# Gated linear attention with an ELU feed-forward: two windows in one visit, four-quadrant products from window 6, loads without the zero rows, and a new issue order of the start

## The chip, the cores and the metric

The kernel runs on one core of a Trainium2 chip. The time is that of the device in microseconds (us) for one execution; a kernel's time is the median of its runs. The core has five engines with queues of their own: TensorE (PE), VectorE (DVE), ScalarE (ACT), GpSimd (POOL) and SyncE (SP), which only issues transfers (DMA) here. Each engine works its instructions in the order in which they were issued, and waits on semaphores for the others.

## The reference

There are 4 batches with 8 heads, 768 steps and a head size of 48. For each head a 48 x 48 state is decayed by a gate per row, gets the outer product of k and v, and is read with q. The outputs of the 8 heads stand side by side as 384 numbers for each of the 3072 tokens, and go through a feed-forward layer with 2048 hidden units.

```python
for t in range(S):
    state = alpha[:, :, t, :, None] * state + np.einsum('bhd,bhe->bhde', k[:, :, t], v[:, :, t])
    y[:, :, t] = np.einsum('bhd,bhde->bhe', q[:, :, t], state)
...
h = x @ w_in
g = np.where(h > 0.0, h, alpha * (np.exp(np.minimum(h, 0.0)) - 1.0))
return (g @ w_out).astype(np.float32)
```

In the second part alpha is 1, so g is the ELU of h.

## The kernel before

**Attention in windows.** The 768 steps of a batch are cut into 6 windows of 128 steps, 24 windows in all. Two heads share the 128 partitions (rows 0 to 47 and 64 to 111; the rows between are zeros), and four such pairs stand side by side, so a window's q, k and gate are one tile of 128 partitions (`qka`), one load (token L; the first two windows in two pieces, LA and LB). A scan on DVE (SC) multiplies the gates up, ACT takes the logarithm and the exponent of it (LN, EX), k and q are scaled (KA, KB, KC, SQ on DVE or POOL). Keys are transposed (TP on PE and KN on ACT in the first windows, T, TA, TB on DVE later). Inside a window there are two chunks of 64 steps. PE computes the scores of each chunk (S), DVE masks them (MK); PE computes the products of keys and values (U), DVE subtracts them from the state (UA, UB) and decays it for the next window (UC); PE computes the outputs y (Y, in the first four windows with YL and Y3), which take both the scores and the state.

**Quarters.** S and U exist in two forms. In the old one a matmul contracts over 128 partitions against operands that hold zeros for the other head (ZS writes such zeros, V0 loads them). In the form with quarters (`S4`, `U4`) four small matmuls work on four 64 x 64 quadrants; each window then has two PSUM banks (`q4`) with U in the first part and S behind it. `QU` and `QS` say from which window the form is used.

**Feed-forward.** Two windows make a block of 256 tokens; there are 12 blocks. y is written to `xt` as a high and a low part in a reduced fp32 form (XH on ACT, XL on DVE; XD is a small transfer that moves the fourth pair's rows). The 2048 hidden units are cut in 8 pieces j. For each block b and piece j, A(b, j) is 18 matmuls of 128x256 into a PSUM bank `h`, ACT and DVE make the ELU (RA, RB, RC) and its high and low part (GH on ACT, GL on DVE), and O(b, j) is 12 matmuls of 128x384 into two banks that are kept over all j; Z copies them out and stores them.

**Weights.** They come as 64-bit words in 16 pieces (F). DVE decodes them (DA, DB, DC, one each for a pair of pieces), ACT writes the high part (WH), DVE or POOL the low part (WL; the list `WLV` says which pieces are DVE's; two pieces go over PE, WP). CA and CB read them again for a check (LC loads). This goes on during the first 70 to 80 us, between the first windows and blocks.

**Order.** Every operation is a token, and the tokens are issued one after the other. `START` is a list, written out by hand, for windows 0 to 9 and for the first three blocks; `steady()` makes the rest from a table of offsets, in which each operation of window i stands at a fixed step n = 4i + offset of the sequence of A's. An engine's queue holds its instructions in that order. All PSUM tiles (eight banks) come from one pool in turn, so a new `h` or a new pair of banks waits until the last reader of the bank's former tile is done. `X.n` are n matmuls on constants whose result is not used; 12 stand ahead of everything.

## Time and profile before

| | |
|---|---|
| median of 3 runs | 513.34 us (511.15 to 514.16) |
| the profiled execution | 510.82 us, span 509.1 us, mean granted clock 0.997 |
| PE busy | 499.0 us, 98% |
| DVE busy | 394.3 us, 77% |
| ACT busy | 301.5 us, 59% |
| POOL busy | 123.2 us, 24% |
| DMA | 61.53 MB in 22724 packets |

The span is the time from the first to the last instruction; the profiled execution's own time is longer by what lies around it. A line in the profile such as `L643 DVE SCALAR_TENSOR_TENSOR h<-r,h ... x96 | 66.1, 693 | 51.1 <-ACT r L638 50.5` is a group: line of the kernel, engine, operation, output and inputs with their shapes, how often; then busy us, mean ns of one; then idle us of the engine just ahead of them and what ended most of it. The chain of waits is the work that ended last, followed back from the end. In the timeline each row has its start, its length and how many equal instructions are in it. The lines on which the prediction rests stand there.

### The profile page before, as it was taken

The numbers are of one execution on the slowest core, as the hardware profiler recorded it, in microseconds if no ns is written. First come the engines' busy times: TensorE is split into PE (matmuls) and PEld (weight loads), VectorE is DVE, ScalarE is ACT, GpSimd is POOL, SyncE is SP. The second block draws the span as 40 slices with busy tenths as digits, with TensorE's granted clock in tenths as the row PEclk, the third lists the DMA queues.
The fourth block names the chain that finished last, engine by engine and source line by source line (L and its number), as shares of the span: only waits on it lengthen the run. The fifth ranks groups of instructions, "written<-read, shape, count | busy, mean of one in ns | idle before, by whom it ended". The sixth has DMA issues, their size and how long they took to land.

```text
span 509.1 us, 13170 instructions
## 1 busy us (share of the span) xinstructions
PE 499.0 (98%) x5404; PEld 482.5 (95%) x5404; DVE 394.3 (77%) x801; ACT 301.5 (59%) x689; POOL 123.2 (24%) x115
## 2 busy tenths in 40 slices
...
GB/s 311 403 410 382 188 1 215 13 120 76 119 102 1 133 148 54 158 121 77 164 102 94 165 79 117 164 72 124 160 74 127 71 66 37 72 40 1 31 4 36
DMA packets 22724, 61.53 MB, mean 121 GB/s; under 512 B 2944, under 2 KB 10112, under 8 KB 22656
## 3 DMA queue, kind: packets, MB, share of 16 engines
...
q8 instruction: 44, 0.72, 0.6%
...
q14 instruction: 24, 0.20, 0.1%
HBM read 53.92 MB, written 4.72 MB: 115 GB/s over the span
## 4 chain that ended last, share of the span: by engine, by line
PE 95%; DMA 3%; SPq 1%; issue 1%; DVE 0%; ACT 0%
PE h L625 41%; PE o L676 40%; PE y L428 4%; DMA vs<-in_vv_dram 3%; PE sc L318 2%; PE q L346 2%; PE u L362 1%; PE y L423 1%; PE q L303 1%; PE wp L112 1%; PE tp L259 0%; SPq L535 0%; PE y L467 0%; PE yl L423 0%; SPq L174 0%
## 5 line engine op out<-in xcount | busy, mean ns | idle before, releaser
L625 PE MATMUL h<-xt,w 128*128 128x256 f32 x1728 | 221.4, 282 | 0.0
L625 PEld LDWEIGHTS h<-xt,w 128*128 128x128 f32 x1728 | 214.0, 188 | 1.5
L676 PE MATMUL o<-w,gh 128*128 128x384 f32 x768 | 198.4, 339 | 0.0
L676 PEld LDWEIGHTS o<-w,gh 128*128 128x128 f32 x768 | 135.6, 188 | 0.2
L676 PE MATMUL o<-w,gl 128*128 128x384 f32 x384 | 129.9, 338 | 0.0
L649 ACT CAST gh<-h 128x512 fp32r<-128x512 f32 x96 | 56.3, 587 | 88.3 <-DVE h L643 71.7
L643 DVE SCALAR_TENSOR_TENSOR h<-r,h 128x512 f32<-128x512 f32 x96 | 66.1, 693 | 51.1 <-ACT r L638 50.5
L633 ACT ACTIVATE r<-h 128x512 f32<-128x512 f32 x96 | 56.7, 594 | 75.1 <-PE h L625 73.5
L238 POOL TENSOR_TENSOR st<-qka,P 64x512 f32<-64x512 f32 x36 | 42.9, 1190 | 212.0 <-issue 166.5
L662 DVE TENSOR_TENSOR gl<-h,gh 128x512 fp32r<-128x512 f32 x96 | 66.1, 690 | 34.2 <-ACT gh L649 33.0
L269 DVE STREAM_TRANSPOSE kn<-qka 32x128 f32<-32x128 f32 x288 | 87.1, 302 | 4.1
L676 PEld LDWEIGHTS o<-w,gl 128*128 128x128 f32 x384 | 72.1, 188 | 0.0
L638 ACT ACTIVATE r<-r 128x512 f32<-128x512 f32 x96 | 60.5, 633 | 2.5
L192 DVE TENSOR_TENSOR_SCAN P<-qka,first 128x516 f32<-128x516 f32 x24 | 29.6, 1237 | 2.3 <-DMA qka<-in_qka_dram 1.5
L214 POOL TENSOR_TENSOR qka<-qka,R 128x512 f32<-128x512 f32 x18 | 23.9, 1330 | 12.5 <-ACT R L206 12.4
L219 POOL TENSOR_TENSOR R<-P,R 128x512 f32<-128x512 f32 x19 | 24.7, 1300 | 5.0 <-DVE qka L214 3.9
L330 DVE TENSOR_TENSOR st<-q,mask 64x256 f32<-64x256 f32 x52 | 22.0, 422 | 1.0
L428 PEld LDWEIGHTS y<-st,vs 128*64 128x64 f32 x576 | 18.3, 138 | 4.2 <-issue 4.0
L581 ACT ACTIVATE ck<-ck,lim 128x384 f32<-128x384 f32 x32 | 20.9, 653 | 1.0
L428 PE MATMUL y<-st,vs 128*64 128x64 f32 x576 | 20.7, 225 | 0.0
L201 ACT ACTIVATE R<-P 128x512 f32<-128x512 f32 x24 | 15.1, 633 | 8.4 <-DVE P L192 8.4
L576 ACT ACTIVATE ck<-ck 128x384 f32<-128x384 f32 x32 | 18.2, 568 | 0.1
(105 smaller groups left out, 418.5 us busy)
## 6 DMA issues: line engine op xcount, KB each, us to landing
...
```

What stands on the lines that cost most here:

```text
L192: nc.vector.tensor_tensor_scan(out=P.rearrange("p n w -> p (n w)"), data0=t[:, 2 * NP * W:], data1=first.rearrange("p n w -> p (n w)"), in ...
L219: eng(KBV, i).tensor_tensor(out=d["R"], in0=pw(i), in1=d["R"], op=ALU.mult)
L238: eng(SQV, i).tensor_tensor(out=st[r, a], in0=d["q"][r], in1=pw(i)[r], op=ALU.mult)
L269: nc.vector.transpose(out=kn[32 * t:32 * t + 32, :, 32 * g:32 * g + 32], in_=d["kt"][32 * g:32 * g + 32, :, 32 * t:32 * t + 32])
L428: nc.tensor.matmul(out[64 * a:64 * a + m], lhsT=lhs(i, c, a)[:, n * D:n * D + m], rhs=d["st"][:, a, n, c * C:(c + 1) * C], start=start, st ...
L625: nc.tensor.matmul(h[:, f, :], lhsT=t[:, wi, ws], rhs=x[:, c, xi, :], start=(f == 0 and k == 0), stop=(k == 8), skip_group_check=True)
L633: nc.scalar.activation(out=r, in_=d["h"], func=AF.Relu, scale=-1.0)
L638: nc.scalar.activation(out=d["r"], in_=d["r"], func=AF.Exp, scale=-1.0)
L643: nc.vector.scalar_tensor_tensor(out=d["h"], in0=d["r"], scalar=-1.0, in1=d["h"], op0=ALU.add, op1=ALU.max)
L649: nc.scalar.copy(out=gh, in_=d["h"])
L662: nc.vector.tensor_tensor(out=gl, in0=d["h"], in1=d["gh"].bitcast(F32), op=ALU.subtract)
L676: nc.tensor.matmul(o[:, 0:DM], lhsT=gt[:, f, ms], rhs=t[:, wi, f * DM:f * DM + DM], start=(j == 0 and f == 0 and k == 0), stop=(j == NJ - ...
```

## The change

Five things are changed together.

- The steady order is a list for one block (`STEADY`) instead of a table of offsets for one window: numbers in it are relative to the block's first A (A.0 of block g) and its first window. Per block there is one visit with y of both windows, and one with U, S, U, S of the next two windows, instead of y, U, S once for each window.
- Quarters start with window 6 instead of 10 for U and 11 for S. S then lies beside its own window's U in one pair of banks from window 10 on (`PAIRS`, `shared`), where before it lay behind U of the window ahead of it.
- From window 3 on a load moves rows 0 to 47 and 64 to 111 only, as two transfers; the three tiles are fixed, and the other rows keep the zeros of windows 0 to 2.
- From window 10 on, every fourth window's masked scores lie in the buffer in which the weights were decoded.
- `START` has a new order for windows 0 to 9, and it reaches further, to O.3.2 instead of O.2.6. Two of WL's pieces, one KA, one KB and one SQ go from DVE to POOL. Both `X.2` are gone.

```diff
--- before.py
+++ after.py
@@ -32,9 +32,11 @@
 WARM = 12
 
 
-QU, QS, SHARE = 10, 11, 11
-
-WLV, KAV, KBV, SQV = (1, 3, 9, 10, 12), (0, 1, 3, 6, 7, 10), (0, 1, 2, 3, 8), (1, 3, 4, 5)
+QU, QS = 6, 6
+
+PAIRS = 10
+
+WLV, KAV, KBV, SQV = (6, 11, 14), (0, 1, 2, 3, 4), (0, 1, 2, 3), (0, 1, 3)
 
 
 WPE, XPE, GPE, UPE = (0, 2), (0, 1), (), (1,)
@@ -43,32 +45,44 @@
 
 
 START = """
-LA.0 SC.0 X.2 LB.0 LN.0 EX.0 LA.1 SQ.0 LB.1 KA.0 KB.0 SC.1 SQ.1 F.0 F.2 KC.0 LN.1 EX.1 LV.1 KA.1 LV.0 S.0 KB.1
-TP.0 KC.1 L.2 PC.0 TP.1 KN.1 KN.0 L.3 PC.1 DA.0 DB.0 S.1 DC.0 U.0 WH.0 U.1 UC.0 X.2 UA.0 UP.1 SC.2 WP.0 F.6
-WH.2 LN.2 SQ.2 MK.1 F.4 LV.3 F.1 UC.1 SC.3 UA.1 EX.2 MK.0 WP.2 DA.2 F.3 YL.1 KA.2 L.5 YL.0 LV.2 KB.2 KC.2 F.9
-LN.3 Y3.1 Y.1 EX.3 DB.2 Y3.0 KA.3 PC.2 KB.3 Y.0 WL.0 XH.1 LC.0 S.2 F.11 TP.2 XP.1 XH.0 KN.2 XP.0 SQ.3 KC.3
-DC.2 TP.3 DA.1 U.2 XL.1 KN.3 U.3 DB.1 WL.2 DC.1 WH.4 UB.2 XL.0 F.5 S.3 L.4 PC.3 A.0.0 UA.2 WH.6 WH.1 UC.2 F.10
-A.0.1 CA.0 WL.6 A.0.3 MK.2 UB.3 UA.3 WH.3 MK.3 UC.3 WL.4 RA.0.0 YL.2 F.7 LV.5 RB.0.0 YL.3 RA.0.1 Y3.2 SC.4
-WL.1 Y3.3 F.12 SC.5 SQ.4 DA.3 WL.3 LN.5 Y.2 LN.4 RB.0.1 SQ.5 F.8 Y.3 RC.0.0 EX.4 EX.5 F.14 A.0.2 RC.0.1 XH.3
-XH.2 L.7 XL.3 XL.2 GH.0.0 GH.0.1 KA.4 GL.0.0 DA.5 DB.3 KA.5 KB.5 DC.3 CB.0 LV.7 V0.7 LV.6 V0.6 RA.0.2 RA.0.3
...
+LA.0 SC.0 LN.0 EX.0 LA.1 SC.1 LB.0 LB.1 KA.0 LN.1 EX.1 SQ.0 KB.0 KC.0 KA.1 KB.1 TP.0 F.0 F.2 KC.1 LV.0 SQ.1
+DA.0 S.0 PC.1 LV.1 LV.2 TP.1 DB.0 S.1 KN.1 L.2 PC.0 KN.0 L.3 U.0 DC.0 UC.0 SC.2 F.4 UA.0 WH.0 MK.0 F.6 U.1
+LV.3 UP.1 WP.0 YL.0 MK.1 UC.1 UA.1 LN.2 SC.3 EX.2 Y3.0 YL.1 F.12 KA.2 KB.2 KC.2 Y3.1 Y.0 LN.3 F.3 SQ.2 WH.2
+Y.1 F.1 SQ.3 EX.3 XH.0 KA.3 XP.0 TP.2 PC.2 F.7 XH.1 WP.2 L.4 KN.2 KB.3 KC.3 XL.0 DA.2 XP.1 LV.5 DB.2 F.5 DC.2
+U.2 DA.1 XL.1 WL.0 S.2 L.5 WH.6 A.0.0 F.11 DB.1 UA.2 UB.2 TP.3 MK.2 UC.2 WH.4 SC.4 WL.2 S.3 KN.3 A.0.1 U.3
+DA.3 WL.4 F.10 RA.0.0 F.9 LN.4 RB.0.0 MK.3 UA.3 DC.1 YL.2 Y3.2 A.0.2 YL.3 DB.3 EX.4 DC.3 RA.0.2 KA.4 Y3.3 WL.6
+PC.3 UB.3 WH.1 Y.2 SQ.4 XH.2 RB.0.2 WH.7 KB.4 F.14 Y.3 XH.3 UC.3 A.0.3 KC.4 ZV.6 TP.4 LV.4 SC.5 SQ.5 XL.3 S.4
+KN.4 WH.3 XL.2 DA.5 RC.0.2 F.8 RC.0.0 DB.5 GH.0.2 LN.5 U.4 EX.5 UB.1 L.7 L.6 RA.0.3 WH.5 GL.0.2 WL.1 RA.0.1
...
+"""
+
+
+STEADY = """
+A.-3 Y.1 XH.1 Y.0 XH.0 A.-2 XL.1 RA.-3 O.-5 RA.-2 XL.0 LV.4 U.2 CA.-12 V.0 RB.-3 S.2 UA.2 MK.2.0 U.3 UB.2 S.3
+MK.2.1 UC.2 XD.1 ZV.4 O.-4 XD.0 RC.-3 CB.-12 SC.4 RB.-2 A.-1 PC.3 GH.-3 RC.-2 A.0 LN.4 GL.-3 UA.3 EX.4 RA.-1
+GH.-2 LC.-11 MK.3.0 L.6 MK.3.1 UB.3 CA.-11 A.1 RA.0 KA.4 L.5 RB.-1 GL.-2 RC.-1 A.2 RB.0 UC.3 CB.-11 RA.1 GH.-1
+RC.0 O.-3 KB.4 RB.1 SC.5 KC.4 LC.-10 GL.-1 LN.5 GH.0 EX.5 RC.1 T.4.1 O.-2 A.3 VP.0 CA.-10 T.4.2 GL.0 GH.1 A.4
+T.4.3 KA.5 O.0 RA.2 GL.1 RB.2 RA.3 CB.-10 LV.5 RC.2 PC.4 GH.2 KB.5 RB.3 GL.2 LC.-9 O.1 O.-1 KC.5 RA.4 O.2 SQ.4
+T.5.2 CA.-9 RB.4 RC.3 CB.-9 RC.4 GH.3 T.5.1 GH.4 T.5.0 GL.3 T.4.0 T.5.3 LC.-8 SQ.5 Z.-1 GL.4
 """
 
 @with_exitstack
@@ -149,13 +163,19 @@
         return win[i]["P"][:, :, 1:]
 
 
+    NQ = 3
+    qka_t = [work.tile([128, QW], F32, name=f"qka{i}", tag=f"qka{i}", bufs=1) for i in range(NQ)]
+
     def qtile(i):
-        t = win[i]["t"] = work.tile([128, QW], F32, name="qka", tag="qka", bufs=3)
+        t = win[i]["t"] = qka_t[i % NQ]
         return t
 
+
     @tok
     def L(i):
-        nc.sync.dma_start(out=qtile(i), in_=qka[i, :, 0:QW])
+        t = qtile(i)
+        for r in [slice(0, 128)] if i < NQ else [slice(0, D), slice(64, 64 + D)]:
+            nc.sync.dma_start(out=t[r], in_=qka[i, r, 0:QW])
 
     @tok
     def LA(i):
@@ -230,7 +250,13 @@
     @tok
     def SQ(i):
         d = win[i]
-        st = d["st"] = work.tile([128, 2, NP, W], F32, name="st", tag="st", bufs=3)
+        if i >= PAIRS and i % 4 == 3:
+
+            st = work.tile([128, 2, WCH], F32, name="st", tag="wm", bufs=1)
+            st = st.rearrange("p a x -> p (a x)")[:, 0:2 * NP * W].rearrange("p (a n w) -> p a n w", a=2, n=NP)
+        else:
+            st = work.tile([128, 2, NP, W], F32, name="st", tag="st", bufs=3)
+        d["st"] = st
         if i < EARLY:
             eng(SQV, i).tensor_tensor(out=st[:, 0], in0=d["q"], in1=pw(i), op=ALU.mult)
         for a in range(2 if i >= EARLY else 0):
@@ -288,20 +314,25 @@
         nc.scalar.copy(out=kn, in_=d["tp"].rearrange("p n (a x) -> p n a x", a=2))
 
 
-    def banks(i):
-        return [psa.tile([128, 512], F32, name="q", tag="pa") for _ in range(2)]
+
+    def shared(i):
+        d = win[i]
+        if i < PAIRS or "q4" not in d:
+            d["q4"] = [psa.tile([128, 512], F32, name="q", tag="pa") for _ in range(2)], set()
+        return d["q4"]
 
     QUADS = ((0, 0), (1, 1), (0, 1), (1, 0))
 
     def S4(i):
         d = win[i]
-        q4 = win[i - 1]["q4"] if i >= SHARE else banks(i)
+        q4, begun = shared(i)
         d["s4"] = [t[:, NP * D:NP * (D + C)].rearrange("p (n t) -> p n t", n=NP) for t in q4]
         for n in range(NP):
             for a, c in QUADS:
                 r, cs = slice(64 * a, 64 * a + D), slice(c * C, (c + 1) * C)
                 nc.tensor.matmul(d["s4"][a][64 * c:64 * c + 64, n, :], lhsT=d["kt"][r, n, cs], rhs=d["st"][r, a, n, cs],
-                                 start=(n == 0 and (i < SHARE or a == 1 and i % NW == 0)), stop=True, skip_group_check=True)
+                                 start=(n == 0 and a not in begun), stop=True, skip_group_check=True)
+        begun.update((0, 1))
 
     @tok
     def S(i):
@@ -338,13 +369,15 @@
 
     def U4(i):
         d = win[i]
-        d["q4"] = banks(i)
-        d["u"] = [t[:, 0:NP * D].rearrange("p (n e) -> p n e", n=NP) for t in d["q4"]]
+        q4, begun = shared(i)
+        d["u"] = [t[:, 0:NP * D].rearrange("p (n e) -> p n e", n=NP) for t in q4]
         for n in range(NP):
             for x, a in QUADS if i % NW < NW - 1 else QUADS[::2]:
                 r = slice(64 * x, 64 * x + 64)
                 nc.tensor.matmul(d["u"][x][64 * a:64 * a + 64, n, :], lhsT=d["kn"][r, n, a, :],
-                                 rhs=d["vn"][r, 2 * n + a, :], start=(n == 0), stop=True, skip_group_check=True)
+                                 rhs=d["vn"][r, 2 * n + a, :], start=(n == 0 and x not in begun), stop=True,
+                                 skip_group_check=True)
+        begun.update((0, 1) if i % NW < NW - 1 else (0,))
 
     @tok
     def U(i):
@@ -730,60 +763,29 @@
     general(ctx, tc, ident, [t[:, 0] for t in wgts], [t[:, 1] for t in wgts], flag[0], qka, vn, wgt, out)
 
 
-def steady(n0=25):
-
-
-    LEFT = dict(T=11)
-    p, late = [], [divmod(n, NJ) for n in range(n0 - 2, n0)]
-
-    def at(n, start, *names):
...
-    p, late = [], [divmod(n, NJ) for n in range(n0 - 2, n0)]
-    for n in range(n0, NBLK * NJ):
-        b, j = divmod(n, NJ)
-        at(n, -22, "L", "LV")
-        at(n, -7, "Y")
-        at(n, -11, "U")
-        at(n, -15, "S")
-        p.append(("A", b, j))
...
-        second(*late.pop(0))
...
+def steady(g0=4):
+
+
+    p, steps, last = [], dict(A=29, RA=29, RB=29, RC=29, GH=29, GL=29, O=27), NBLK * NJ
+    for g in range(g0, g0 + 10):
+        for x in STEADY.split():
+            x, k, *y = x.split(".")
+            if x in steps:
+                k = NJ * g + int(k)
+                if steps[x] <= k < last:
+                    p.append((x, *divmod(k, NJ)))
+            elif x in ("CA", "CB", "LC"):
+                k = 4 * g + int(k)
+                if 4 + (x == "LC") <= k < 4 * NJ:
+                    p.append((x, k))
+            elif x == "Z":
+                if g0 - 1 <= g + int(k) < NBLK:
+                    p.append((x, g + int(k)))
+            elif x in ("V", "VP"):
+                if g == NBLK - 1:
+                    p.append((x,))
+            elif 2 * g + int(k) < NWIN:
+                p.append((x, 2 * g + int(k), *map(int, y)))
     return p
 
 
```

`X.2` no longer appears: before it stood twice in `START`, behind SC.0 and behind UC.0.

**The start on PE.** Names: `wd` are the two rounds of a weight's low part (WP.0 and WP.2), `yl` and `y` the outputs of windows 0 and 1, `tp` transposed keys, `sc` scores, `u` state products, `h` the first A. Before, from the end of the second weight round on:

```order
L598 MATMUL wd<-wm,ident 128x384
L486 MATMUL wd<-w_233,minus 128x384
L423 MATMUL yl<-st,vs_106 64x64 x8
L423 MATMUL yl<-st,vs_105 64x64 x6
L467 MATMUL y<-y_319,sel 64x128 x6
L423 MATMUL y<-st,vs_106 48x64 x24
L467 MATMUL y<-y_354,sel 64x128 x6
L423 MATMUL y<-st,vs_105 48x64 x18
L318 MATMUL sc<-st,qka 64x64 x16
L259 MATMUL tp<-ident,qka 128x128 x4
L486 MATMUL y<-xt,minus 128x384 x2
L259 MATMUL tp<-ident,qka 128x128 x4
```

and now, from the end of those y to the first A and behind it:

```order
L456 MATMUL y<-st,vs_106 48x64 x24
L519 MATMUL y<-xt,minus 128x384
L285 MATMUL tp<-ident,qka_125 128x128 x4
L631 MATMUL wd<-wm,ident 128x384
L519 MATMUL wd<-w_238,minus 128x384
L631 MATMUL wd<-wm,ident 128x384
L519 MATMUL wd<-w_238,minus 128x384
L519 MATMUL y<-xt,minus 128x384
L395 MATMUL u<-vs_107,kn 64x48 x16
L349 MATMUL sc<-st,qka_125 64x64 x16
L658 MATMUL h<-xt,w_238 128x256 x18
L285 MATMUL tp<-ident,qka_123 128x128 x4
```

The second weight round moved behind the y groups, and the transposes, scores and products of window 3 moved behind the first A. Before, U and S of windows 2 and 3 and both `tp` stood ahead of it.

**The loads on SP.** `vs_107` is the v of window 2, `raw` are weight pieces, `qka` the windows. Before:

```order
L535 DMA raw_146<-in_wgt_dram 128x1536 x2
L174 DMA vs_106<-in_vv_dram 128x768
L174 DMA vs_105<-in_vv_dram 128x768
L158 DMA qka<-in_qka_dram 128x1540 x2
L535 DMA raw_266<-in_wgt_dram 128x1536 x2
L174 DMA vs_108<-in_vv_dram 128x768
L535 DMA raw_276<-in_wgt_dram 128x1536 x2
L158 DMA qka<-in_qka_dram 128x1540
L174 DMA vs_107<-in_vv_dram 128x768
```

and now:

```order
L568 DMA raw_154<-in_wgt_dram 128x1536 x2
L194 DMA vs_105<-in_vv_dram 128x768
L194 DMA vs_106<-in_vv_dram 128x768
L194 DMA vs_107<-in_vv_dram 128x768
L178 DMA qka_125<-in_qka_dram 128x1540
L178 DMA qka_123<-in_qka_dram 48x1540 x2
```

The v of window 2 now stands right behind those of windows 0 and 1, and window 3's load is two transfers of 48 rows.

**The steady order on PE.** `q` are the banks of U and S with quarters, `y` outputs, `h` an A, `o` an O (twelve matmuls, in the rows as two and one in turn). Before, the end of an O and what stands between it and the next O, which is so for every window:

```order
L676 MATMUL o<-w_802,gl 128x384
L428 MATMUL y<-st,vs_108 64x64 x16
L346 MATMUL q<-vs_105,kn 64x48 x16
L303 MATMUL q<-st,qka 64x64 x16
L625 MATMUL h<-xt,w_926 128x256 x18
L676 MATMUL o<-w_802,gh 128x384 x2
```

Now the first visit of a block, and (behind an A and an O) the second:

```order
L658 MATMUL h<-xt,w_949 128x256 x18
L461 MATMUL y<-st,vs_108 64x64 x16
L461 MATMUL y<-st,vs_107 64x64 x16
L658 MATMUL h<-xt,w_1096 128x256 x18
L709 MATMUL o<-w_636,gh 128x384 x2
L709 MATMUL o<-w_636,gl 128x384
```

```order
L709 MATMUL o<-w_636,gl 128x384
L377 MATMUL q<-vs_105,kn 64x48 x16
L333 MATMUL q<-st,qka_124 64x64 x16
L377 MATMUL q<-vs_106,kn 64x48 x8
L333 MATMUL q<-st,qka_125 64x64 x16
L709 MATMUL o<-w_834,gh 128x384 x2
```

The y of one window, its successor's U and the next S stood together once a window; now two windows' y stand together, and then two windows' U and S.

75 lines of the change are left out of this document (20 added, 55 removed).

## The prediction

> **What bounds the kernel now.** First the busy times and the chain of waits that ended last.
>
> ```profile
> PE 499.0 (98%) x5404; PEld 482.5 (95%) x5404; DVE 394.3 (77%) x801; ACT 301.5 (59%) x689; POOL 123.2 (24%) x115
> ...
> PE 95%; DMA 3%; SPq 1%; issue 1%; DVE 0%; ACT 0%
> ```
>
> TensorE (PE) is busy 98% of the span and is 95% of the chain; VectorE (DVE) has 77%. So only PE time counts: fewer or shorter matmul groups, or less PE idling. The chain names the pieces (start, duration, what).
>
> ```profile
> 17.10 12.96 DMA vs<-in_vv_dram
> ...
> 33.89 6.54 PE h L625 x54
> ...
> 85.51 4.23 PE h L625 x36
> ...
> 98.20 2.06 PE y L423 x64
> ...
> 199.64 1.08 PE y L428 x32
> ...
> 206.25 2.14 PE h L625 x18
> ...
> 216.91 2.12 PE o L676 x12
> 219.04 1.08 PE y L428 x32
> ```
>
> The first hidden product (A, `h`) begins at 33.9 us behind a v load that took 13 us. In the steady part a period of one window is 219.04 − 199.64 = 19.40 us, all PE. The profiled run took 510.82 us (span 509.1). I make the sum against that run and carry the difference to the median 513.34; the 2.5 us between them is taken to stay.
>
> **The change part by part.**
>
> *Quarters from window 6 instead of 10.* Scores (S) and state products (U) then use four 64x64 quadrants. The timeline shows both forms, a window without quarters and a later one with them:
>
> ```profile
> 136.06 0.53 PE L362 MATMUL u<-vs,kn 128*48 128x48 f32 x16
> ...
> 136.78 1.12 PE L318 MATMUL sc<-st,qka 128*64 128x64 f32 x32
> 137.82 1.44 PE L625 MATMUL h<-xt,w 128*128 128x256 f32 x10
> ...
> 220.05 0.68 PE L346 MATMUL q<-vs,kn 64*64 64x48 f32 x32
> 220.55 0.66 PE L303 MATMUL q<-st,qka 48*64 48x64 f32 x32
> 221.14 1.10 PE L625 MATMUL h<-xt,w 128*128 128x256 f32 x7
> ```
>
> U: 136.78 − 136.06 = 0.72 against 220.55 − 220.05 = 0.50 (start to start). S: 1.04 against 0.59. The old form of S is used up to window 10, so five windows gain 0.45 and four gain 0.22 on U: 2.25 + 0.9 = 3.15; I take **−3.0**. The mask of a window then takes four short DVE operations instead of two long ones, and one subtraction is added per window; that is DVE time beside A and O matmuls, and costs nothing while DVE keeps ahead (below); with that cover gone it is at most the four masks of a window, 4 × 0.42 = 1.7 us, five times.
>
> *Two windows in one visit.* Two y groups behind each other take 2.06 (row 98.20, x64), apart 2 × 1.08: −0.10. The second thing is where A stands: two A's behind each other take 4.23 (2.115 each, row 85.51), an A behind another kind 2.14; the list of two windows has four A's behind an A: −0.10. Eight periods of two windows: **−1.6**. U and S in one visit instead of two change nothing that a row shows; I leave it at zero, with ±0.1 a period.
>
> *Waits that the visit can make.* In the new list PE runs y y, A, O, u s u s, O, A A A A. Scores and state products of both windows fill the PSUM banks that the next A's want, and DVE empties them. Durations of DVE's part:
>
> ```profile
> L643 DVE SCALAR_TENSOR_TENSOR h<-r,h 128x512 f32<-128x512 f32 x96 | 66.1, 693 | 51.1 <-ACT r L638 50.5
> L662 DVE TENSOR_TENSOR gl<-h,gh 128x512 fp32r<-128x512 f32 x96 | 66.1, 690 | 34.2 <-ACT gh L649 33.0
> L192 DVE TENSOR_TENSOR_SCAN P<-qka,first 128x516 f32<-128x516 f32 x24 | 29.6, 1237 | 2.3 <-DMA qka<-in_qka_dram 1.5
> ...
> L330 DVE TENSOR_TENSOR st<-q,mask 64x256 f32<-64x256 f32 x52 | 22.0, 422 | 1.0
> L381 DVE TENSOR_TENSOR vs<-vs,q 48x192 f32<-48x192 f32 x24 | 8.4, 348 | 0.3
> ```
>
> After the first window's scores PE still has u (0.50), s (0.59), O (2.12) and 0.10 of hand-over to issue: 3.31 us to the third A. DVE needs for the first window's banks two L381 (0.70), two masks (0.84), two more subtractions like L381 (0.70) and two masks (0.84): 3.08, and a hand-over on each side. So the margin is about +0.2 less the two hand-overs, of which no row gives the length: a stall from 0 to 0.2. For the second window's banks DVE needs 3.08 + 0.70 + 2 × 0.69 (L643) + 1.24 (L192) + 0.69 (L662) + 0.70 + 1.69 = 9.5 us, while PE has 3.31 + 2.14 + 2 × 2.115 = 9.68: again just in time. What waits behind a late DVE: PE issues in order, so a late bank holds the four A's and with them every O. I charge 0.1 a period, 8 periods: **+0.8**, bounds 0 and +3.
>
> *First A earlier, but less work ahead of it.* The timeline of PE before the first A:
>
> ```profile
> 18.61 0.81 PE L598 MATMUL wd<-wm,ident 128*128 128x384 f32 x2
> ...
> 21.98 1.08 PE L423 MATMUL yl<-st,vs 48*64 48x64 f32 x28
> ...
> 27.26 1.14 PE L318 MATMUL sc<-st,qka 48*64 48x64 f32 x32
> 28.32 0.66 PE L259 MATMUL tp<-ident,qka 128*128 128x128 f32 x4
> ...
> 30.19 2.69 PE L362 MATMUL u<-vs,kn 128*64 128x48 f32 x61 [0.42 <-DMA vs<-in_vv_dram]
> ```
>
> The v of window 2 moves from the 14th to the 9th place in SP's queue with five loads fewer ahead of it, so the wait of 0.42 and what was queued behind the load go. The two rounds of weight parts (18.61 to 21.98) take 1.69 each; one of them moves behind the y groups, which then end at 27.26 − 1.69 = 25.57. Behind them stand 0.42 (transposes, 28.74 − 28.32), 1.69, twice 0.22 (y·minus, by the 0.43 between 28.74 and 29.17), U of window 2 (1.25, half of the 2.48 from 30.19) and S (1.06): first A at 30.4 instead of 33.9. But window 3's transposes, S and U (0.42 + 1.06 + 1.25 = 2.7) now come after it. Net **−0.7**. Dropping four of the 16 warm matmuls removes work from a stretch in which PE waits, and counts nothing. Bounds: −2 and +1.5, the last if the y groups wait for the new load order.
>
> *Start phase, DVE.* From 30 to 60 us DVE, not PE, has no reserve (columns: stretch, its length, then PE, PEld, DVE, ACT, POOL busy, the clock, DMA share, GB/s):
>
> ```profile
> 30.00:40.00 10.00, 9.75 (x148) 9.48 (x149) 9.19 (x13) 7.44 (x15) 4.90 (x2) 1.00 1.02 412
> 40.00:50.00 10.00, 10.00 (x188) 9.29 (x187) 9.39 (x14) 7.14 (x20) 4.21 (x3) 1.00 1.02 393
> 50.00:60.00 10.00, 10.00 (x104) 9.77 (x104) 9.96 (x11) 5.73 (x10) 4.38 (x2) 1.00 0.97 251
> ```
>
> The new order puts other DVE work ahead of the first low part (GL.0.0), on which the first O rests. Before:
>
> ```profile
> 47.86 0.69 DVE L662 TENSOR_TENSOR gl<-h,gh 128x512 fp32r<-128x512 f32 x1
> ...
> 58.62 0.52 PE L676 MATMUL o<-w,gh 128*128 128x384 f32 x2
> ```
>
> ```profile
> L557 DVE SCALAR_TENSOR_TENSOR spare<-raw,spare 128x1536 int32<-128x1536 int32 x4 | 7.5, 1865 | 0.0
> L557 DVE SCALAR_TENSOR_TENSOR wm<-raw,wm 128x1536 int32<-128x1536 int32 x4 | 7.0, 1752 | 0.1
> L609 POOL TENSOR_TENSOR w<-wm,w 128x768 fp32r<-128x768 f32 x5 | 11.0, 2202 | 26.2 <-ACT w L589 26.2
> ...
> L609 DVE TENSOR_TENSOR w<-spare,w 128x768 fp32r<-128x768 f32 x4 | 3.8, 947 | 0.0
> ```
>
> Twelve instructions come ahead of it: four long decode ones (1.75 each), one of about 1.05, one L609 (0.95) and six of about 0.69: 13.1 us. Five leave: two L609 and three of 0.69: 4.0. So it ends at 48.55 + 9.1 = 57.7, or at 56.3 if DVE's idle time in the first two stretches (0.81 + 0.61) is filled. PE reaches the first O at 30.4 + 26.5 = 56.9: the 24.8 us between rows 33.89 and 58.62, plus 2.7 (window 3's work) and 1.2 (U of window 4), less one A (2.2). The stall there is 0 to 0.8 us; the ten us of lead that DVE had are gone, and whatever DVE delivers next (weights for the next A's) is as tight. I take **+0.5**, bounds 0 and +3.3 (below).
>
> *Loads without the zero rows* (577.5 instead of 770 KB, two issues instead of one) the scores of every fourth window in a buffer that the decode left free, and the S and U of one window in one pair of banks: DMA is free from 60 us on, and every window's load is ahead by more than a period, and the order in which a pair's U and S come is not tied tighter; cost zero, hidden by PE; a late load shows as a wait of the scan, L192, which before waited 1.5 us in all.
>
> Sum: −3.0 − 1.6 + 0.8 − 0.7 + 0.5 = **−4.0**: 506.8 for a run like the profiled one, **509.3** for the median.
>
> **Rivals.**
>
> *Start phase bound by DVE.* For it: the rows of 30 to 60 us, and the margin of ±0.8 us at the first O. Against it: two L609 and three small ones leave DVE for GpSimd (POOL), 4 us. If DVE ends at 57.7 the first O stalls 0.8; the two pieces of w that POOL takes over take 2.20 instead of 0.95, and an A that waits for each waits 1.25 longer: 3.3 in place of 0.5, so 512.1.
>
> *DVE and POOL in each other's way.* The decode instruction took 1.87 us in one buffer and 1.75 in the other, while POOL worked. If each of the two extra POOL pieces (2.20) holds DVE for its whole length, +4.4 less the 1.9 DVE saves = +2.5: 511.8 as well. [...] The rows above show 0.11 us on average, much less than a whole lock, so the rival gets a small chance.
>
> *Slower: the double visit.* One mechanism: both windows' banks come free late because DVE reaches the first subtraction behind low parts that wait for ACT (L662 waits 33 us in all for it). It decides from a stall of (3.0 + 1.6 + 0.7 − 0.5)/8 = 0.6 us a period. One L662 with its wait of 0.34 (33.0/96) and a 0.2 hand-over come late: 1.2 us, 8 × 1.2 = +9.6 in place of +0.8: +4.8, 518.1. For it: margins of 0.2 at two places. Against: DVE is busy only 77% of the span, so 0.23 × 38.8 = 9 us of a period of two windows are idle.
>
> *The clock.* PE is thinly used around 8 to 15 us, and the granted clock (last but two columns) falls there:
>
> ```profile
> 8.20:11.60 3.40, 1.28 (x29) 1.31 (x31) 3.21 (x5) 2.02 (x5) 0.00 (x0) 0.86 1.00 415
> 11.60:15.00 3.40, 3.40 (x49) 2.91 (x45) 3.33 (x4) 1.01 (x3) 0.00 (x0) 0.64 1.02 401
> ```
>
> With four warm matmuls fewer PE idles longer, and one more stretch of 3.4 us at half speed costs up to 1.7: 511.0. [...]
>
> **How the numbers follow.** A measurement of this kernel tells 0.5% from no change, so faster is below 510.8 and slower above 515.9. Forecast 0.50 (its own range 506.5 to 511), start phase 0.20, port 0.08, slower visit 0.14, clock 0.08. Faster: 0.48 of the forecast, 0.04 each of start phase and clock, 0.01 of the port: 0.57. Slower: 0.13 of the visit and 0.02 of the start phase: 0.15. Same: the rest, 0.28. The range: with no wait in either place (−1.3), −2 in place of −0.7 at the first A, and −0.1 a period for the visit (−0.8) it is 509.3 − 3.4, about 506.0; upward it is the start phase (512.1) with +0.8 in place of −0.7 at the first A, 513.6. Left out are the slower visit and little else.
>
> **What would show it.** Right: U and S of windows 6 to 9 at 0.50 and 0.59; first A near 30.4; a period of two windows of 38.7 us with two y groups in 2.06; no idle of PE over 0.2 at the third A of a period. Start-phase rival: PE idle with releaser DVE between 55 and 70 us, and DVE at 10.0 of 10 there. Port: L557 and L662 longer while L609 runs on POOL. Slower visit: PE idle before `h` with releaser L361 (the mask) each period. Clock: below 0.9 in a stretch after 15 us. Wrong altogether: a PE total that does not fall by the 3 us of the quarters.

## The result, and the profile after

The changed kernel takes 517.08 us (median of 8 runs, 514.88 to 518.62) where the kernel before took 513.72 beside it: a ratio of 1.0073, 95% interval 1.0043 to 1.0102. It is slower by three quarters of a per cent; the forecast was 509.3 and faster. The profiled execution took 518.29 us (span 516.5, mean granted clock 0.978).

The busy times, and the shares of the chain that ended last, from the page of the changed kernel:

```profile
PE 501.1 (97%) x5400; PEld 484.2 (94%) x5400; DVE 391.1 (76%) x808; ACT 288.9 (56%) x689; POOL 127.9 (25%) x110
...
PE 85%; DMA 6%; DVE 4%; issue 2%; POOL 1%; ACT 1%; SPq 0%; DVEq 0%; POOLq 0%
```

PE has less to do than before and is still busy 2.1 us longer, because a part of it ran at half clock (0.50 from 11.8 to 22 us, in the rows below); and it stood idle 15.4 us of its span instead of 10.1. The chain is no longer 95% PE: transfers and DVE have come into it. Its early pieces (start, duration, what):

```profile
14.23 10.08 DMA raw<-in_wgt_dram
24.38 15.71 DMA qka<-in_qka_dram
40.21 1.24 DVE P L212
```

The load of window 4 took 15.7 us from its issue, and the scan of that window, on DVE, waited for it. The tables by stretch show why; the columns are stretch, length, busy PE, PEld, DVE, ACT, POOL, then the granted clock, the DMA share and GB/s. Before:

```profile
11.80:15.20 3.40, 3.38 (x47) 2.80 (x45) 3.33 (x4) 1.21 (x3) 0.00 (x0) 0.67 1.02 393
15.20:18.60 3.40, 3.40 (x70) 3.04 (x71) 3.20 (x4) 2.11 (x5) 0.00 (x0) 1.00 0.99 392
...
39.00:42.40 3.40, 3.40 (x61) 3.02 (x61) 3.40 (x4) 0.82 (x3) 0.00 (x0) 1.00 1.01 402
42.40:45.80 3.40, 3.40 (x101) 3.15 (x102) 3.34 (x6) 2.61 (x7) 1.27 (x1) 1.00 1.03 415
```

and after:

```profile
11.80:15.20 3.40, 3.40 (x50) 2.95 (x48) 3.37 (x4) 1.49 (x4) 0.00 (x0) 0.50 1.05 426
15.20:18.60 3.40, 3.40 (x60) 3.10 (x58) 2.35 (x3) 0.91 (x3) 0.00 (x0) 0.50 1.06 225
18.60:22.00 3.40, 3.40 (x37) 3.22 (x34) 2.56 (x4) 1.05 (x2) 1.18 (x1) 0.50 0.98 249
...
39.00:42.40 3.40, 3.40 (x62) 3.09 (x61) 1.23 (x1) 0.92 (x2) 0.82 (x1) 1.00 1.01 240
42.40:45.80 3.40, 2.24 (x18) 2.03 (x18) 0.89 (x2) 1.60 (x5) 0.36 (x1) 1.00 1.04 250
45.80:49.20 3.40, 2.42 (x28) 2.06 (x28) 3.40 (x5) 1.27 (x4) 0.00 (x0) 0.66 0.98 372
```

Two things are new. In the stretches in which windows are loaded the DMA engines are as busy as ever (share about 1.0) and move 225 to 250 GB/s instead of 390 to 415. And the granted clock is 0.50 for ten us (11.8 to 22) where before it was 0.67 for 3.4 us. Not all of this second difference is the change's: the profiled execution of the kernel before has a mean clock of 0.997, a value that 13 of its 72 executions beside the experiments reach (0.996 or more), and that of the changed kernel has 0.978, the lowest of its eight. At 39 to 46 us DVE, which had no reserve before, is nearly idle. Its timeline there tells for whom it waits (start, length, and in brackets the idle time ahead and what ended it):

```profile
40.21 1.23 DVE L212 TENSOR_TENSOR_SCAN P<-qka,first 128x516 f32<-128x516 f32 x1 [1.59 <-DMA qka<-in_qka_dram]
44.91 0.96 DVE L584 TENSOR_SCALAR wm<-raw 128x1536 int32<-128x1536 int32 x1 [3.46 <-DMA raw<-in_wgt_dram]
45.78 0.68 DVE L366 TENSOR_TENSOR st<-sc,mask 128x512 f32<-128x512 f32 x1
46.38 0.35 DVE L414 TENSOR_TENSOR vs<-vs,u 128x192 f32<-128x192 f32 x1
```

The decode of a weight pair (DA.3) waited for its piece until 44.91, and the mask and the state of window 3 stood behind it in DVE's queue. PE wanted that state for an output:

```profile
46.78 1.11 PE L456 MATMUL yl<-st,vs 48*64 48x64 f32 x16 [2.15 <-DVE vs L414]
```

A second loss stands at 123 us. PE's timeline, and then that of SP's queue of transfers:

```profile
119.72 1.16 PE L333 MATMUL q<-st,qka 48*64 48x64 f32 x64
120.81 0.62 PE L709 MATMUL o<-w,gh 128*128 128x384 f32 x2
...
125.13 3.89 PE L658 MATMUL h<-xt,w 128*128 128x256 f32 x18 [1.94 <-DVE st L361]
128.94 0.68 PE L377 MATMUL q<-vs,kn 64*64 64x48 f32 x32
129.56 0.62 PE L658 MATMUL h<-xt,w 128*128 128x256 f32 x3
```

```profile
111.37 0.54 SPq L197 DMA_DIRECT2D vs<-in_vv_dram  x1
117.84 0.86 SPq L720 DMA_DIRECT2D out_dram<-ot  x2
118.74 0.48 SPq L196 DMA_DIRECT2D vs<-in_vv_dram  x1
119.26 0.59 SPq L197 DMA_DIRECT2D vs<-in_vv_dram  x1
120.36 1.31 SPq L548 DMA_DIRECT2D xt<-y  x2
```

The A that starts at 125.13 is A.2.1, the first of block 2 in the new order. It also needs the small transfer XD.5 (L548), which SP issued only at 120.36, behind the stores of Z.0 and a load, though its data were ready at 113.4. The idle time was followed by half clock (0.50 granted from 126 to 128 us): this A took 3.8 us instead of 2.1.

In the steady part the change did what it should, and more. The y pairs there, four periods of two windows apart:

```profile
267.24 2.02 PE y L461 x64
...
421.09 2.02 PE y L461 x64
```

(421.09 − 267.24)/4 = 38.46 us a period, against 2 × 19.41 = 38.82 before.

### The profile page after: what moved, and what is told of

Its sections match the earlier page's. It is cut to its first block, busy times and chain, and to the rows that moved or that the text cites. A ratio compares the mean times of both kernels' runs of the same rounds, so it can differ in the third digit from the quotient of the medians.

```text
span 516.5 us, 13313 instructions
## 1 busy us (share of the span) xinstructions
PE 501.1 (97%) x5400; PEld 484.2 (94%) x5400; DVE 391.1 (76%) x808; ACT 288.9 (56%) x689; POOL 127.9 (25%) x110
## 4 chain that ended last, share of the span: by engine, by line
PE 85%; DMA 6%; DVE 4%; issue 2%; POOL 1%; ACT 1%; SPq 0%; DVEq 0%; POOLq 0%
PE o L709 39%; PE h L658 37%; DMA qka<-in_qka_dram 4%; PE y L461 4%; DMA raw<-in_wgt_dram 2%; PE q L377 2%; PE q L333 2%; PE y L456 1%; DVE st L361 1%; PE sc L349 1%; DVE P L212 0%; DVE kn L295 0%; DVE spare L596 0%; DVE spare L590 0%; DVE h L676 0%
## 5 line engine op out<-in xcount | busy, mean ns | idle before, releaser
L658 PE MATMUL h<-xt,w 128*128 128x256 f32 x1728 | 217.3, 283 | 1.9 <-DVE st L361 1.9
L658 PEld LDWEIGHTS h<-xt,w 128*128 128x128 f32 x1728 | 211.3, 190 | 4.0 <-issue 2.2
L666 ACT ACTIVATE r<-h 128x512 f32<-128x512 f32 x96 | 56.9, 596 | 55.0 <-PE h L658 52.2
L676 DVE SCALAR_TENSOR_TENSOR h<-r,h 128x512 f32<-128x512 f32 x96 | 64.4, 688 | 15.4 <-ACT r L671 14.6
L671 ACT ACTIVATE r<-r 128x512 f32<-128x512 f32 x96 | 59.1, 632 | 0.6
L361 DVE TENSOR_TENSOR st<-q,mask 64x256 f32<-64x256 f32 x72 | 30.4, 422 | 10.8 <-ACT vs L412 9.2
L239 POOL TENSOR_TENSOR R<-P,R 128x512 f32<-128x512 f32 x20 | 25.1, 1257 | 11.2 <-DVE qka L234 9.8
L221 ACT ACTIVATE R<-P 128x512 f32<-128x512 f32 x24 | 15.2, 633 | 22.6 <-DVE P L212 22.6
L414 DVE TENSOR_TENSOR vs<-vs,q 48x192 f32<-48x192 f32 x30 | 10.5, 349 | 21.3 <-PE q L333 17.0
L514 ACT ACTIVATE y<-y 128x128 fp32r<-128x128 f32 x20 | 5.6, 278 | 29.7 <-PE y L461 27.5
L642 POOL TENSOR_TENSOR w<-spare,w 128x768 fp32r<-128x768 f32 x6 | 16.0, 2674 | 19.7 <-ACT w L622 19.6
## 6 DMA issues: line engine op xcount, KB each, us to landing
raw<-in_wgt_dram SPq DMA_DIRECT2D x16, 768.0 KB, 13.1
```

The source lines that it names most:

```text
L239: eng(KBV, i).tensor_tensor(out=d["R"], in0=pw(i), in1=d["R"], op=ALU.mult)
L361: nc.vector.tensor_tensor(out=d["st"][r, a, :, c * C:(c + 1) * C], in0=d["s4"][a][o], in1=mask[o].unsqueeze(1).broadcast_to([64, NP, C]), ...
L658: nc.tensor.matmul(h[:, f, :], lhsT=t[:, wi, ws], rhs=x[:, c, xi, :], start=(f == 0 and k == 0), stop=(k == 8), skip_group_check=True)
L666: nc.scalar.activation(out=r, in_=d["h"], func=AF.Relu, scale=-1.0)
L671: nc.scalar.activation(out=d["r"], in_=d["r"], func=AF.Exp, scale=-1.0)
L676: nc.vector.scalar_tensor_tensor(out=d["h"], in0=d["r"], scalar=-1.0, in1=d["h"], op0=ALU.add, op1=ALU.max)
```

## The experiments

All times are medians; the kernel before stood at 513.0 to 513.2 beside each of them.

**1. Whole rows.** The theory: the loads in two parts of 48 rows run at half the rate (225 to 250 GB/s where the other rows have 390 to 415) and make everything behind them late. The rival: it is the new order of the transfers (a weight piece that is issued earlier now).

```diff
-        for r in [slice(0, 128)] if i < NQ else [slice(0, D), slice(64, 64 + D)]:
+        for r in [slice(0, 128)]:
             nc.sync.dma_start(out=t[r], in_=qka[i, r, 0:QW])
```

> The changed kernel, but each window is again loaded as one transfer of 128 rows (770 KB) instead of two of 48. Theory L (the two-part loads halve the transfer rate, and the v and weight pieces behind them come late): in the changed kernel the stretches 16 to 20 and 32 to 46 us moved 180 to 290 GB/s at a DMA share of 1.0, where the others moved 400 to 420; with whole rows both are near 400, the fourth window's load and the weight pieces behind it land about 6 us earlier, PE's idle time between 42 and 49 us (2.1 us) and the slow clock behind it (1.4 us) go: 517.1 - 3.5 = 513.6 (512 to 515). Rival, order of the transfers (a weight piece issued earlier than before is what stands ahead): the whole rows carry more bytes, the same idle time stays, 517 (516.5 to 519).

Measured: 510.21 us, 6.9 less than the changed kernel and ratio 0.9928 to the kernel before (0.9902 to 0.9955). That is twice the gain expected. 3.0 us of it stand at the first O (62.2 against 65.2 us), and 2.7 more come until the seventeenth (144.1 against 149.8), where the wait for XD.5 became shorter and no half clock followed it (1.00 granted from 120 to 130 us); PE's waits in this run name that transfer now:

```profile
PE h L658 <- DMA xt<-y: 1.4, 1, 1.4
```

The stretches of this run:

```profile
15.20:18.60 3.40, 3.40 (x60) 3.10 (x58) 2.35 (x3) 0.79 (x3) 0.00 (x0) 0.50 0.98 382
18.60:22.00 3.40, 3.40 (x34) 3.19 (x32) 2.48 (x5) 1.05 (x2) 1.18 (x1) 0.50 1.01 409
...
39.00:42.40 3.40, 3.40 (x54) 3.20 (x51) 3.20 (x5) 1.28 (x3) 2.00 (x2) 1.00 0.99 408
42.40:45.80 3.40, 3.40 (x55) 3.20 (x52) 3.22 (x4) 1.23 (x4) 0.49 (x1) 1.00 1.03 421
```

The rate is back at 380 to 420 GB/s although a third more bytes are loaded, DVE works through 39 to 46 us, and PE doesn't wait. The order of transfers is the changed kernel's, so the rival falls. The clock is still 0.50 to 0.53 from 8.4 to 25.4 us, and the first A came later than in the changed kernel, at 35.16 us.

**2. The four unused matmuls put back.** 

```diff
-LA.0 SC.0 LN.0 EX.0 LA.1 ...
+LA.0 SC.0 X.2 LN.0 EX.0 LA.1 ...
-... U.0 DC.0 UC.0 SC.2 F.4 ...
+... U.0 DC.0 UC.0 X.2 SC.2 F.4 ...
```

> The changed kernel with the four unused matmuls of the old start put back (two behind the first scan, two behind the first state update). Theory L: the PE's slow stretch (clock 0.50 from 10 to 22 us) ends some 7 us earlier and the first A starts 3 to 4 us earlier, near 31; but the wait for the late weight piece and load at 42 to 45 us stays where it is, so most is lost again: 516.5 (515.5 to 517.5), and the idle time at 42 to 49 us grows by about as much. Rival, clock alone: the excess of slow work, 4.3 us, comes back in full: 512.8 (512 to 514).

Measured: 516.96. No gain; but the run doesn't show what it was made for, since the clock stayed low as long as in the changed kernel (0.50 from 11.8 to 22 us), and the first A came at 34.45 instead of 34.21 us. With two matmuls there the clock fell in this execution; with sixteen it was 1.00 in the same stretches (runs 5, 9 to 11).

**3. XD.5 ahead of Z.0.** The theory: A.2.1 waits for XD.5. The rival: for the mask of window 6, which the profile names as what ended the wait.

```diff
-O.0.7 XL.5 UC.6 LV.9 ...
+O.0.7 XL.5 XD.5 UC.6 LV.9 ...
-MK.6 XD.5 A.2.1 RB.1.7 ...
+MK.6 A.2.1 RB.1.7 ...
```

> The changed kernel with the small transfer XD.5 (rows of y of window 5) issued right behind XL.5, ahead of the stores Z.0 and the load LV.8 on SP's queue. Theory X (A.2.1 at 123.2 us waits for XD.5, which stood behind Z.0 on SP until 120.4 and took 4 us to land): PE's idle 1.94 us at 123 to 125 and the half clock behind it (about 1.5 us) go: 517.1 - 3.4 = 513.7 (513 to 515). Rival, the mask (the profile names the mask of window 6 as what ended that wait, at 125.1): the idle time stays: 517 (516 to 518).

Measured: 515.34, 1.7 less. The idle time ahead of A.2.1 is gone with nothing changed on DVE, so the wait was the transfer's and not the mask's. Half of the gain is missing: PE waits elsewhere now, as the waits of PE in this run (us in total, times, longest) show in its third and fourth rows, which the changed kernel didn't have.

```profile
PE tp L285 <- issue: 2.2, 1, 2.2
PE wp L126 <- DVE first L120: 2.1, 1, 2.1
PE q L377 <- issue: 1.1, 1, 1.1
PE h L658 <- DVE w L642: 0.8, 1, 0.8
```

**4. All three edits.**

> The three edits together: whole rows, the four unused matmuls, XD.5 ahead of Z.0. If the losses are those three and independent: 517.1 - 3.5 - 4.3 - 3.4 = 505.9 (505 to 508.5), about 1.4% faster than the kernel before. If DVE, busy 9 to 10 of 10 from 50 us on, bounds the start phase instead: some 4 us of it are lost again, 510 (508.5 to 513), with PE idle behind DVE between 50 and 70 us.

Measured: 510.44, ratio 0.9935 (0.9908 to 0.9962): no better than whole rows alone, and the second guess of the two. But its reason, DVE from 50 us on, was not the one: the clock was 0.50 to 0.55 from 12 to 25 us in this run too, and the first A came at 35.6 us. So the clock's gain, one of the three expected, had not come in this execution. The other executions hint at its size: two of the twelve had a mean clock of 0.997 and 0.998 and took 506.64 and 506.47 us, the other ten had 0.981 to 0.987 and took 509.74 to 511.27.

**5. Sixteen unused matmuls instead of two.** As run 4, with the hole in PE's work from 6.7 to 10.3 us filled.

```diff
-LA.0 SC.0 X.2 LN.0 EX.0 ...
+LA.0 SC.0 X.16 LN.0 EX.0 ...
```

> As the run with all three edits (whole rows, XD.5 ahead, unused matmuls), but with 16 unused matmuls behind the first scan instead of two, so that PE has no idle time from 6.7 to 10.3 us. In that run the granted clock was 0.50 to 0.55 from 12 to 25 us, and DVE stood idle 4.4 us in sum at 20 to 28 us behind PE's slow products (UP.1, Y.0). Theory C1 (the idle stretch starts the slow clock): the clock stays at 1.0 from 8 to 25 us, the first A starts near 31 instead of 35.6, the first O near 58.5 instead of 62.6: 510.4 - 3.5 = 506.9 (505.5 to 508.5). Theory C2 (the small products of the first two windows are too light a load to hold the clock up): it falls to 0.5 all the same, some us later, and the time stays, 510.4 (509.5 to 512).

Measured: 506.92 us, ratio 0.9885 to the kernel before (0.9854 to 0.9915). This is the fastest version: 1.15% faster than before, 10.2 us faster than the change. The stretches:

```profile
8.40:11.80 3.40, 2.66 (x38) 1.66 (x38) 3.30 (x6) 0.00 (x0) 0.00 (x0) 1.00 1.01 418
11.80:15.20 3.40, 2.42 (x60) 1.96 (x56) 3.37 (x4) 2.40 (x6) 0.00 (x0) 1.00 1.03 419
15.20:18.60 3.40, 3.24 (x66) 2.76 (x64) 3.28 (x4) 0.82 (x2) 0.00 (x0) 1.00 1.02 412
```

The clock stays at 1.00, and PE then has time to spare where it was "busy" throughout at half clock. All six executions have a mean clock of 0.997 or more, so the matmuls make the rule what was the exception in run 4. The first A starts at 31.38 us, the first O at 58.4.

**6. The loads alone, on the kernel before.** The first try took the three tiles by the window's number. The kernel before issues window 5's load ahead of window 4's, so that load took the tile from which window 2 was still to be read: other data were computed with, and further waits came in.

```diff
-        t = win[i]["t"] = work.tile([128, QW], F32, name="qka", tag="qka", bufs=3)
+        t = win[i]["t"] = qka_t[i % NQ]
...
-        nc.sync.dma_start(out=qtile(i), in_=qka[i, :, 0:QW])
+        t = qtile(i)
+        for r in [slice(0, 128)] if i < NQ else [slice(0, D), slice(64, 64 + D)]:
+            nc.sync.dma_start(out=t[r], in_=qka[i, r, 0:QW])
```

> The kernel before, with only the loads changed: from window 3 on two transfers of rows 0 to 47 and 64 to 111 instead of one of 128 rows. Theory L (the two-part loads halve the rate while the queue is full): stretches near 200 to 250 GB/s at a DMA share of 1.0 before 60 us; five window loads each keep the queue 2.9 us instead of 1.9, so weights and v land 3 to 5 us later, and PE, which waited for v of window 2 already, starts its first A some 2 to 4 us later: 513.2 + 3 = 516 (514.5 to 518). Rival (the loads hurt only together with the new order of transfers): 513 (512 to 514).

It took 524.19 us, which says nothing on the question. The second try takes the tiles in the order of the loads:

```diff
-        t = win[i]["t"] = qka_t[i % NQ]
+        t = win[i]["t"] = qka_t[len(loaded) % NQ]
+        loaded.append(i)
```

> The kernel before with the loads changed alone: from the fourth load on two transfers of rows 0 to 47 and 64 to 111, into three fixed tiles taken in the order of the loads, as its pool did (the run e6 took them by the window's number, so that the load of window 5, which this kernel issues ahead of window 4's, stood in the tile that window 2 still used). Theory L: the queue is full until 58 us, the five window loads of that stretch each take about 1 us longer, v of window 2 (which the first A waits for) and the weight pieces land 2 to 4 us later: 513.0 + 3 = 516 (514.5 to 519). Rival (the loads hurt only with the new order of transfers): 513 (512 to 514).

Measured: 516.47, ratio 1.009 (1.0058 to 1.0122). The loads alone cost the kernel before 3.4 us; the rival (only together with the new order) falls. The rate in this run, at the same places:

```profile
15.20:18.60 3.40, 3.40 (x56) 3.02 (x53) 2.45 (x3) 1.51 (x5) 0.00 (x0) 0.50 1.01 241
39.00:42.40 3.40, 3.27 (x28) 3.07 (x28) 1.23 (x4) 1.59 (x3) 1.80 (x1) 1.00 1.02 245
```

The clock is low here as well, 0.50 in the first row, with the old kernel's two warm matmuls in place: with those two alone it had not recovered by 18.6 us in this execution.

**7. Two transfers of 64 rows.** Is it the odd count of 48 rows, or that a transfer goes to one half of the partitions?

```diff
-        for r in [slice(0, 128)] if i < NQ else [slice(0, D), slice(64, 64 + D)]:
+        for r in [slice(0, 128)] if i < NQ else [slice(0, 64), slice(64, 128)]:
```

> The changed kernel, with two transfers of 64 rows each (0 to 63, 64 to 127) for a window: all bytes again, but still in two parts. Theory P (a transfer that goes to one half of the partitions has half the rate, whatever its size): stretches near 200 to 250 GB/s at a DMA share of 1.0 as in the changed kernel, and the parts take 48/64 more: 519 (517 to 522). Rival R (48 rows are an unlucky count, or rows are too few): 400 GB/s as with whole rows, 510.5 (509.5 to 512).

Measured: 519.61, ratio 1.0137 (1.0095 to 1.0179), as the theory of the halves had it. The rate:

```profile
15.20:18.60 3.40, 2.71 (x69) 2.43 (x66) 2.43 (x3) 1.54 (x5) 0.00 (x0) 1.00 1.03 257
39.00:42.40 3.40, 3.40 (x63) 3.15 (x62) 1.23 (x1) 1.41 (x4) 1.18 (x1) 1.00 1.04 248
```

Exactly the same bytes as with whole rows, in two halves, at 0.6 to 0.7 of the rate: 257 and 248 GB/s against 382 and 408 in run 1. The clock is no part of this: it was 1.00 in both of these rows (and 0.81 and 0.69 in the two stretches from 22 to 28.8 us). The run agrees with the theory of the halves, and the second half, issued right behind the first, does not make up for it.

**8. One transfer of 112 rows**, with XD.5 moved as in run 3.

```diff
-        for r in [slice(0, 128)] if i < NQ else [slice(0, D), slice(64, 64 + D)]:
+        for r in [slice(0, 128 if i < NQ else 64 + D)]:
```

> The changed kernel with XD.5 ahead of Z.0 and one transfer of rows 0 to 111 for a window from window 3 on (674 KB; 16 rows of zeros left out instead of 32). Theory P: the transfer goes to both halves, its rate is near 400 GB/s, and the time that of whole rows with the same edit, about 510.0 (509 to 511.5). Rival R (any transfer of fewer than 128 rows is slow): the stretches near 200 GB/s are there again and the time is that of the changed kernel with XD.5 ahead, 515 (514 to 517).

Measured: 512.92, ratio 1.0003 (0.9983 to 1.0023). The time lies between both guesses, 2.4 us below run 3 and 2.5 above run 4; the rate in these stretches is near the rival's:

```profile
15.20:18.60 3.40, 3.40 (x60) 3.10 (x58) 2.33 (x3) 0.84 (x3) 0.00 (x0) 0.50 1.03 266
39.00:42.40 3.40, 3.40 (x53) 3.14 (x50) 1.92 (x3) 1.43 (x3) 2.01 (x2) 1.00 1.02 239
```

So going to both halves was not enough for the 382 and 408 GB/s of whole rows, and what makes 112 rows slow stays open: the theory of the halves doesn't cover it, and that every transfer of fewer than 128 rows is slow would fit runs 7 and 8 alike. What is shown are the rates in these two stretches: 382 and 408 GB/s with 128 rows, 266 and 239 with 112, 257 and 248 with twice 64, 225 and 240 with twice 48. Leaving out zero rows saved bytes and lost time in every form that was tried: 6.9 us with twice 48 (run 1), 2.5 with 112 (run 8 against run 4).

**9 to 11. The clock and XD.5, each in another setting.** Sixteen matmuls with the 48-row loads; sixteen on the kernel before; whole rows and sixteen without moving XD.5. Their diffs are those shown above.

> The changed kernel with its 48-row loads, plus 16 unused matmuls behind the first scan and two behind the first state update. If the late transfers bound this kernel's start, as the 2 us wait for the weight piece at 42 to 45 us says, PE gains its 3 to 4 us before 35 us and waits them away at 40 to 46 us: 516 (515 to 517.3). If the slow clock costs what it holds PE up, whatever the loads do, the gain of the whole-row version (510.4 to 506.9) comes here too: 513.6 (512.8 to 514.6).

> The kernel before with 16 instead of two unused matmuls behind the first scan. Its own slow stretch is one of 3.4 us at 11 to 14 us, and its first A waits for the v of window 2, which lands at 30.06 us: no gain, 513.0 (512.3 to 513.8). If instead the slow clock costs it time as it does the changed kernel with whole rows, 1.7 us: 511.3 (510.5 to 512).

> The changed kernel with whole rows and 16 plus two unused matmuls, XD.5 left where the change put it (behind Z.0 on SP): tells what moving XD.5 is worth once the other two are mended. If A.2.1 waits for it as in the run with whole rows alone (1.4 us of PE): 506.9 + 1.3 = 508.2 (507.5 to 509.5). If DVE is what holds that stretch: 506.9 (506.4 to 507.4).

Run 9: 516.50, only 0.6 less than the changed kernel, so the sixteen matmuls are worth next to nothing while the loads are slow. The rows show how the gain is lost:

```profile
11.80:15.20 3.40, 2.42 (x56) 2.03 (x54) 3.37 (x4) 2.40 (x6) 0.00 (x0) 1.00 1.04 422
...
22.00:25.40 3.40, 2.71 (x43) 2.31 (x41) 2.30 (x4) 2.75 (x8) 0.00 (x0) 0.67 1.01 408
...
42.40:45.80 3.40, 1.34 (x13) 1.14 (x13) 1.95 (x4) 0.60 (x1) 0.00 (x0) 1.00 1.00 294
```

The clock is 1.00 only until 22 us and falls to 0.67 behind some short waits of PE, so the first A comes at 33.37 us, 0.8 earlier than in the changed kernel and not 3 to 4 as expected (31.04 in run 11, the same with whole rows). The rest goes at 42.4 to 45.8, where PE idles 2.1 us.

Run 10: 511.25, ratio 0.9983 (0.9956 to 1.0011). The interval reaches no change, but the time is the second guess's: eleven of the twelve executions had a mean clock of 0.998 or more and took 510.29 to 511.96, as the few executions of the kernel before with a high clock do (five of the 21 beside it had 0.996 or more, 510.63 to 510.88). Its first A came at 33.51 us instead of 33.82.

Run 11: 508.13, ratio 0.9918 (0.9887 to 0.9949). Against run 1 the sixteen matmuls are worth 2.1 us with whole rows, and against run 5 XD.5 is worth 1.2.

The 10.2 us from the changed kernel to run 5 are then: whole rows 6.9, the clock 2.1, XD.5 1.2, taken in this order. The three are not independent, and another order gives other sizes: the clock 3.5 as the last step (run 4 to run 5), whole rows 8.4 with the sixteen matmuls in place (run 9 to run 11), XD.5 1.7 alone (run 3).

## Why the prediction was wrong, step by step

**The loads** (forecast: zero; measured: +6.9) is the step that failed. It said "DMA is free from 60 us on, and every window's load is ahead by more than a period". That holds in the steady part, where a period takes as long with whole rows (38.47 us in run 5, 38.46 in the changed kernel). But the loads of windows 3 to 5 fall before 50 us, and there the prediction's own rows showed a DMA share of 1.02: a full queue, in which what stood behind the loads came late (the decode of DA.3's piece started at 44.91 us, at 40.92 in run 1). I counted bytes (577 against 770 KB) and took the rate as given. The rate fell by 40% (225 and 240 GB/s against 382 and 408 in run 1), so a window's load became longer, not shorter, and the weight pieces behind it were late. The sign that it named, a wait of the scan for its load, did come, but small: 3.0 us in all instead of 1.5.

The profile of the kernel before already held such a stretch; the prediction's row of 50 to 60 us has a DMA share of 0.97 at 251 GB/s. In finer stretches:

```profile
49.20:52.60 3.40, 3.40 (x31) 3.40 (x30) 3.37 (x3) 1.76 (x4) 0.00 (x0) 1.00 1.03 218
52.60:56.00 3.40, 3.40 (x46) 3.23 (x47) 3.40 (x6) 2.37 (x4) 1.83 (x1) 1.00 1.00 230
```

From 46.2 to 50.6 us SP had issued six transfers of v of 64 rows each (L176, L177, L183) and one of 128. Full engines (share 1.03 and 1.00) at little more than half the rate of the other rows (218 and 230 GB/s against 392 to 415) were there to be seen, though no run changes these transfers by themselves.

**What was queued behind the late transfer** was missed too. DA.3 on DVE had window 3's mask and state behind it, and PE's y waited for these. The rival "start phase bound by DVE" looked at the right engine, at another time and with another cause: it named 55 to 70 us and a full DVE, and PE lost its time at 44.6 to 46.8, when DVE was not full but waited. From 56 to 66 us DVE was indeed busy throughout (3.40 of 3.40 us in each stretch), and PE didn't wait for it there by more than 0.1 us.

**The clock** was a rival with a chance of 0.08 and a price of 1.7 us. That a hole in PE's work ahead brings the clock down was right: the hole is 2.5 us long in the kernel before (7.81 to 10.32) and 3.6 in the changed one (6.7 to 10.3), and with it filled the clock stayed at 1.00 through the start in three of four runs, and in the fourth (run 9) until 22 us. That the four dropped matmuls are to blame is not shown: with them put back (runs 2 and 4), and in the old kernel with slow loads (run 6), the clock stayed as low, and 40 of 72 executions of the kernel before have a mean clock of 0.989 or less too. The size was off: 10 us at 0.50, not one more stretch of 3.4, about the length that the kernel before shows (0.50 from 10.8 to 13.8 us, 0.92 and 0.87 in the us on either side). With the loads mended the clock is worth 2.1 to 3.5 us, and with 48-row loads next to nothing (run 9). The **first A** came at 34.21 instead of 30.4; it needed both, whole rows and a clock held up, to come at 31.04 (run 11) and 31.38 (run 5), where whole rows alone gave 35.16 and the clock alone 33.37.

**XD.5** behind Z.0 on SP was in no step. The order of SP's queue was only looked at for the first loads, and what stands there ahead of XD.5 was not counted: 1.2 us in run 11 against run 5, 1.7 in run 3.

**Quarters** (forecast −3.0): right, by two errors that cancel. S of windows 6 and 7 took 120.81 − 119.72 = 1.09 for both, 0.5 less each than the old 1.04, where 0.45 was forecast. U of window 7 took 129.56 − 128.94 = 0.62 against 0.72, and windows 6, 8 and 9 took 0.65, 0.75 and 0.61, so U gave 0.25 us in all and not 0.9. Five times 0.50 and 0.25 are 2.7.

**Steady visits and their waits** (forecast −1.6 and +0.8): right in direction, too timid. A period is shorter by 0.36 us, not 0.10; eight of them are −2.9. The y pair takes 2.02, so 0.14 less than two alone, and no wait for a bank shows at the A's behind the visit: the hand-overs that I feared there did not come to more than the margin. The "slower: double visit" rival is out.

**Start phase, DVE** (forecast +0.5, first O at 56.9): the first O came at 65.2 in the changed kernel, for the reasons above. In run 5 it came at 58.4, 1.0 of the 1.5 us from the later first A, and PE waited 0.4 us in all for the low part (GL), so this term held.

**The sum.** With whole rows and the clock held up (run 11) the kernel takes 508.13, and with XD.5 moved (run 5) 506.92. The forecast to hold beside these is not 509.3 but its 506.8 for an execution like the profiled one. The 2.5 us between the two, "taken to stay", go with the clock: 13 executions of the kernel before with a mean clock of 0.996 or more took 510.85 in the median, 40 with 0.989 or less 513.5. So run 11 is 1.3 us late, about what XD.5 costs, and run 5 is on the forecast, but partly by luck. Quarters and steady visits gave 2.7 and 2.9 us, where 3.0 and 0.8 were forecast; run 5 is 3.9 us faster than the profiled execution of before, so the start still costs some 1.7 us where the forecast had a gain of 0.2. Where these go is not traced. The hand-over of 0.2 us in the price of the slower visit was an assumption; no row gives it.

**DVE and POOL in each other's way**: small, as said. In the changed kernel's chain at 60 to 65 us, with POOL busy throughout:

```profile
59.66 2.11 DVE spare L590
...
62.97 2.15 DVE spare L596
```

The chain shows the larger part of these two decode instructions; in full they took 2.19 and 2.22 us instead of 1.75, so 0.4 to 0.5 longer each, not by the whole length of a POOL instruction (2.95 and 3.38 us there). That a POOL piece holds DVE for its whole length, on which the +4.4 of this rival ("port" in its chances) rests, no run shows; these 0.4 to 0.5 us stand in its place.
